# RWKV-6 and a GELU MLP in one kernel: no products of zeros behind the first tile's level bursts, 24 instead of 8 ahead of them, weights loaded later, all loops in another order

## The chip, the core and the metric

The kernel runs on one core of a Trainium2 chip. The metric is the device time of one execution in microseconds. Before the change three executions took 588.85, 590.56 and 590.85 us, a median of 590.56.

Engines are named as the profile names them: PE is the matrix engine (PEld its weight loads), DVE the vector engine, ACT the scalar engine, POOL the general-purpose engine, SP the engine that issues most transfers. Each engine works through its own queue in order. An engine that waits for another one holds up all that is queued behind it.

## The reference

First comes a recurrent attention block (RWKV-6) over 4 batches, 8 heads, 768 steps and 48 columns, then a two-layer MLP with an exact GELU, on 3072 tokens of width 384 with 2048 hidden columns:

```
for t in range(S):
    cur = einsum('bhd,bhe->bhde', u[None] * k_t, v_t)
    y[:, :, t] = einsum('bhd,bhde->bhe', r_t, state + cur)
    state = w_t[:, :, :, None] * state + einsum('bhd,bhe->bhde', k_t, v_t)
x = y.transpose(0, 2, 1, 3).reshape(B * S, H * D)
h = x @ w_in
g = 0.5 * h * (1.0 + erf(h / sqrt(2)))
out = g @ w_out
```

The inputs r, k, v, w and u are float32. The weights w_in and w_out arrive as 64-bit floats, which the kernel reads as 64-bit words and turns into float32 itself.

## The kernel before, in words

The 3072 tokens are worked in eight tiles of 384 tokens, x = 0 to 7. A tile is half the sequence of one batch, all eight heads. Each tile goes through `attention(x, unit)` and then `mlp(x)`.

In the attention, time is cut into chunks of 64 steps. Inside a chunk the sums over earlier steps are made level by level: at level h (1, 2, 4, 8, 16, 32) PE multiplies r of the later half of each block of 2h steps with k of its earlier half. All of a level's products are written by `products` (L445) into one pair of PSUM banks named `d`; such a group is called a burst here. DVE then multiplies r and k by the decays of that level (L494, L505) and copies the burst's block into the matrix `a_sb` through a mask (L516, and L465 for the diagonal), or ACT copies it (L513) where blocks are 16 steps or longer. After the last level k is transposed (`kt_ps`, L685) and copied by ACT (L687), PE makes each chunk's addition to the state (`kv_ps`, L711) and the part inside the chunk (`y_ps`, L752), DVE carries the state from chunk to chunk (`chain_states`, L726 and L731), `fences` (L762, L764) read the finished banks, and PE adds the part from the state (L797). ACT and DVE copy the result into `xT` (L804, L820), a copy `ysb` (L823) and small transfers (L827) fill the rest of `xT`.

Tile 0 is worked as two units, each with half of the heads, so that one unit's DVE work can lie beside the other's PE work. Tile 1 is one unit. Tiles 2 to 7 use another form of the levels, in quarters (L557 to L671).

In the MLP of tile 0, PE makes h one block of 128 hidden columns at a time (L1059, three products a block, in a pool of two banks). ACT's gelu follows in two instructions (L1062, L1064), and PE multiplies by w_out (L1153). From tile 1 on the products are cut in halves in a Strassen-like way (L929, L1073, sums on DVE at L897 and the lines around L1170 to L1196).

The weights come in 16 pieces: eight of w_in and eight of w_out. A piece is loaded by SP into a buffer `raw` (L200, or in three thirds at L205), ACT takes it apart into two halves (`prepare`: L333, L334, L336), and DVE shifts one half (L345) and adds both into the place of the weights (L349). The `gate` form of the loads writes one element of the buffer on DVE first (L204), which delays the issue of the transfer until DVE gets there. The loads of r, k, w of tile 1 have the same gate (L163, L164). The very first transfers (w, k and r of both units at L150, u, v) are issued ahead of all.

PE also runs products of zeros, 128 x 128 by 128 x 512 in bfloat16, whose result nobody reads (`keep_warm`, L225): eight at the start, two behind each burst of tile 0 but the first of each unit (`rest`), and two times three through the stream `warm()`.

The order of work is written out by hand. Every piece of work is a generator that stops at each `yield`. For each tile a string in `PLAN` names which generator goes on next: in tile 0 "." is unit 0, "s" unit 1, "l" the loads with a gate, "c" the weights' conversions, "p" two conversions on their own, "f" the following tile's attention, "w" the load of v, "x" the zeros of `warm()`. In the later tiles "." is the MLP of the tile before, "s" the attention begun in the loop before, "f" the next one, "l" the loads, "c" the weights (tile 1), "x" and "w" sums for the halves. Each engine's queue has its instructions in the order in which the generators wrote them.

## Time and profile before

| | us |
|---|---|
| median of three runs (588.85 to 590.85) | 590.56 |
| the profiled execution | 589.61 |
| its span, first to last instruction | 587.8 |
| PE busy | 571.1 |
| DVE busy | 425.5 |
| ACT busy | 291.2 |
| PE busy in the first 45 us | 33.2 |
| first product of the MLP (h_ps, L1059) | at 44.40 |
| first product with the last piece of w_out (L1153) | at 110.39 |

The profile's times count from the first instruction of the span. The 1.8 us between span and time lie around it. An entry of the timeline gives the start, the length, engine, line, operation, output and inputs with their shape, the number of records, and in brackets how long the engine had been idle and what it had waited for. A float32 product leaves two records, and a few records are missing (of six products of zeros, five may be shown). An entry of the table by stretches gives each engine's busy time in the stretch with the number of instructions, then the granted clock of PE as a share of full speed, the share of the transfer engines and the rate in GB/s.

### The profile page before, as it was taken

How to read it: one execution, taken by the hardware profiler on the slowest of the kernel's cores; microseconds unless marked ns; L12 is line 12 of the kernel's file. 1: busy time of each engine (PE TensorE's matmuls, PEld its weight loads, DVE VectorE, ACT ScalarE, POOL GpSimd, SP SyncE). 2: the span in 40 equal slices, each digit the busy share in tenths (PEclk: the TensorE clock that was granted, in tenths of full speed). 3: DMA queues.
4: the chain of work that ended last, by engine and by line, in shares of the span. 5: the costliest groups of instructions: out<-in, count | busy, mean ns of one | idle time of the engine just before them, and what ended most of it. 6: DMA issues, size and time to landing. Idle time of an engine off the chain costs nothing. (4 is left out here: it accounts for less than half of the span.)

```text
span 587.8 us, 17656 instructions
## 1 busy us (share of the span) xinstructions
PE 571.1 (97%) x7602; PEld 521.4 (89%) x7616; DVE 425.5 (72%) x825; ACT 291.2 (50%) x668; POOL 58.6 (10%) x63
## 2 busy tenths in 40 slices
PE   5789999999999999999999999999999999999997
PEld 3576666799999999999999999999998999999997
DVE  5988968989758975777959986777759987420332
ACT  2368898446362567235462467245561467335400
POOL 3100000013000130012000130002100111003100
PEclk8999999999999999999999999999999999999999
DMA  6749742253032542354122632344224333114201
GB/s 230 221 135 352 265 168 78 79 142 52 5 89 64 157 58 41 90 142 93 26 55 79 151 70 44 86 139 74 27 41 119 86 42 42 29 45 55 28 13 35
DMA packets 62430, 55.09 MB, mean 94 GB/s; under 512 B 32400, under 2 KB 47504, under 8 KB 62352
## 3 DMA queue, kind: packets, MB, share of 16 engines
q1 hardware_dynamic: 50832, 45.62, 25.5%
q0 software_dynamic: 11424, 8.26, 10.8%
q8 instruction: 60, 0.98, 0.7%
q14 instruction: 18, 0.15, 0.1%
q10 hardware_dynamic: 96, 0.07, 0.1%
HBM read 36.24 MB, written 4.72 MB: 70 GB/s over the span
## 5 line engine op out<-in xcount | busy, mean ns | idle before, releaser
L929 PE MATMUL h_ps<-xT,w_in_sb 128*128 128x192 f32 x560 | 111.5, 330 | 0.6 <-DVE o_sb L1196 0.6
L980 POOL DMA_DIRECT2D g<-o_sb x42 | 50.6, 1229 | 478.2 <-ACT o_sb L965 468.9
L929 PEld LDWEIGHTS h_ps<-xT,w_in_sb 128*128 128x128 f32 x560 | 93.0, 190 | 4.7 <-ACT g L961 1.6
L929 PE MATMUL u_ps<-s,w_in_sb 128*128 128x192 f32 x224 | 41.2, 327 | 0.0
L1073 PE MATMUL o_ps<-w_out_sb,g 128*128 128x192 f32 x224 | 39.8, 326 | 0.0
L929 PEld LDWEIGHTS u_ps<-s,w_in_sb 128*128 128x128 f32 x224 | 37.1, 190 | 0.2
L1073 PEld LDWEIGHTS o_ps<-w_out_sb,g 128*128 128x128 f32 x224 | 37.0, 190 | 0.0
L604 ACT COPY a_sb<-d 32x256 f32<-32x256 f32 (+8 forms) x90 | 32.6, 362 | 4.9 <-PE d L588 3.4
L1059 PE MATMUL h_ps<-xT,w_in_sb 128*128 128x384 f32 x96 | 33.2, 494 | 0.0
L452 PEld LDWEIGHTS d<-rkw 64*64 64x64 f32 x1152 | 19.4, 138 | 14.7 <-issue 10.5
L1073 PE MATMUL o_ps<-w_out_sb,f 128*128 128x192 f32 x176 | 32.0, 331 | 0.0
L1073 PE MATMUL o_ps<-t,g 128*128 128x192 f32 x176 | 31.4, 330 | 0.0
L1073 PE MATMUL o_ps<-t,s 128*128 128x192 f32 x176 | 31.2, 328 | 0.0
L1073 PE MATMUL o_ps<-t,e 128*128 128x192 f32 x176 | 30.6, 326 | 0.5 <-issue 0.5
L621 DVE COPY_PREDICATED a_sb<-quarter,d 128x480 f32<-128x480 uint8 (+5 forms) x54 | 23.2, 439 | 10.5 <-PE d L588 9.3
L726 DVE SCALAR_TENSOR_TENSOR st<-st,tot_sb,kv_ps 128x48 f32<-128x48 f32 x160 | 28.9, 258 | 2.6 <-PE kv_ps L711 2.5
L1073 PE MATMUL o_ps<-w_out_sb,e 128*128 128x192 f32 x176 | 30.7, 328 | 0.0
L982 DVE TENSOR_TENSOR g<-g,o_sb 128x384 f32<-128x384 f32 x14 | 7.6, 549 | 31.2 <-ACT o_sb L965 31.1
L1073 PEld LDWEIGHTS o_ps<-t,e 128*128 128x128 f32 x176 | 28.9, 190 | 0.7 <-issue 0.7
L1073 PEld LDWEIGHTS o_ps<-t,g 128*128 128x128 f32 x176 | 28.6, 190 | 0.5
L1073 PEld LDWEIGHTS o_ps<-w_out_sb,f 128*128 128x128 f32 x176 | 28.5, 190 | 0.6
L1073 PEld LDWEIGHTS o_ps<-t,s 128*128 128x128 f32 x176 | 28.8, 190 | 0.2
(163 smaller groups left out, 1171.3 us busy)
## 6 DMA issues: line engine op xcount, KB each, us to landing
rkw<-in_rkw_dram SPq DMA_DIRECT2D x54, 256.0 KB, 3.6
g<-o_sb POOLq DMA_DIRECT2D x42, 192.0 KB, 3.6
raw<-in_w_out_dram SPq DMA_DIRECT2D x8, 768.0 KB, 6.2
v_in<-in_v_dram SPq DMA_DIRECT2D x8, 584.0 KB, 4.6
raw<-in_w_in_dram SPq DMA_DIRECT2D x5, 768.0 KB, 7.5
out_dram<-o_sb SPq DMA_DIRECT2D x20, 192.0 KB, 2.0
rkw<-kx SPq DMA_DIRECT2D x72, 48.0 KB, 2.0
rkw<-in_rkw_dram SPq DMA_DIRECT2D x6, 384.0 KB, 6.2
```

Of the source, the lines that this page charges most:

```text
L452: nc.tensor.matmul(d[half[p], g, n * width:(n + 1) * width], lhsT=kc[half[g], b, i, p], rhs=right(half[g], b, i, p), start=True, stop=True)
L604: nc.scalar.copy(out=at[z, g, first:behind, (a + 1) * h:], in_=d[z, :, :, to] if g == slice(None) else d[z, :, to])
L621: nc.vector.copy_predicated(out=an[:, :, :, :, (a + 1) * h:], mask=mask.to_broadcast(data.shape), data=data)
L726: nc.vector.scalar_tensor_tensor(out=stq[:, q, c], in0=stq[:, q, c - 1] if c else b4[:, q, NC - 1], scalar=totq[:, q, c:c + 1], in1=kvs[q ...
L929: nc.tensor.matmul(o, lhsT=lhsT, rhs=rhs, start=start, stop=True, skip_group_check=True)
L980: nc.gpsimd.dma_start(out=g, in_=z, accum_op=ALU.add)
L982: nc.vector.tensor_add(g, g, z)
L1059: nc.tensor.matmul(h_ps, lhsT=w_in_sb[:, f // FI, j, f % FI * 128:(f % FI + 1) * 128], rhs=xT[:, j, :], start=(j == 0), stop=(j == NJ - 1))
L1073: nc.tensor.matmul(o, lhsT=lhs(j), rhs=rhs(j), start=start and j == 0, stop=(j == HF - 1), skip_group_check=True)
```

## The change

Three things are edited. `keep_warm(8)` at the start becomes `keep_warm(24)`. `products` no longer writes two products of zeros behind a burst of tile 0, so its argument `rest` goes too. And all eight strings of `PLAN` are replaced: the same steps are written in another order.

```
-    0: "l.s....llsl.lssslslss.lc.l.slslls...ssss..lcs.s.s.l.ss..ss..sccs.c.s.llpssslw..cs.ffpcc",
+    0: "..s...lll..sslsslcl.lllcsls.slsp.l.llss.sss..sl.sss..ssc..s.cs..ssc.sl.l.s.sc.cscs.cffwp",
     1: (
-        "..ccswccc.csl.scscs.s.sccwsc.clccs.ccsccc.csc.lscclswwclc.scs.wcssw.ss.cclcsc.ccs.lclccsc."
-        "ccclfccccccfccfcccccfccfccwf.ff......fw.sl.w.x.wx...x..x...xww"
+        "wl.cwcs.c..sslsccc.ccc.sswsccsc.ccl.csccwsl.scscsssccclc.ssscw.sll.cs..l.l.ccsccccffccsccf"
+        "ccccfc.ccccfcccccc.fc..c..cc..lccwwsx.w.w.x..x.x....xww..w"
     ),
     2: (
-        "s.s.....ss....ssw.ws.wl.wsss.wws.s..lsl...lws.w..s.ww....s.s..l..sss.lssss....s..s..s.sls."
-        "llsf.sf.fs..fl.xx.x.fxx"
+        "sss.lsw.w..s....sw..s.w.l..s.sswsss.wl.....sl.w.slw..sswwss....ssss.sssl.s...s....s...s.ls"
+        ".ssllf..sf.fs.ff..xxl..xfxx"
     ),
...
-    keep_warm(8)
+    keep_warm(24)
...
-        def products(bs, right, width, rest=False):
+        def products(bs, right, width):
             d = pair("d")
...
-            if x == 0 and not rest:
-                keep_warm(2)
             return d[:, :, 0:n * width]
...
-                    d = products(range(np_), lambda z, b, i, p: rc[z, b, i, p], C, h == 1)
+                    d = products(range(np_), lambda z, b, i, p: rc[z, b, i, p], C)
```

On the engines' queues this gives, for tile 0: 24 products of zeros ahead of the first burst, and none between the bursts, in sum eight fewer than before. The gate's write for the first third of piece 0 moves on DVE from ahead of the first decay products (L411) to behind the first pair of L494; those of piece 1 move a few instructions ahead. ACT converts piece 1 (L333 to L336) right behind piece 0, ahead of its copies L513, where it stood behind the second L687. DVE's levels of the two units are interleaved otherwise, both chains of states follow each other directly, and the fence of unit 1 stands behind both. On SP the last third of piece 2 is issued ahead of the transfers of `xT`.

For tile 1: on PE the products of level bursts from `kx` stand between h blocks 0 and 1 instead of 1 and 2, and `kt_ps` and `kv_ps` come two h blocks earlier. On ACT the conversion of piece 3 stands ahead of the gelu of block 1, where it stood behind it, and later conversions move against the gelus in the same way; on DVE the pieces 8 and later are added behind the chain of states.

For tiles 2 to 7 single steps move: in tile 2 ACT's L604 copies go ahead of L1115 and L1118, one DVE product L385 goes ahead of L1189, L1192 and L1196, and the first two groups of the level products at L588 are written ahead of a pair of h products.

More of the change, by code (lines that the diff above doesn't have):

```diff
@@ L39 @@
 PLAN = {
-    0: "l.s....llsl.lssslslss.lc.l.slslls...ssss..lcs.s.s.l.ss..ss..sccs.c.s.llpssslw..cs.ffpcc",
+    0: "..s...lll..sslsslcl.lllcsls.slsp.l.llss.sss..sl.sss..ssc..s.cs..ssc.sl.l.s.sc.cscs.cffwp",
     1: (
-        "..ccswccc.csl.scscs.s.sccwsc.clccs.ccsccc.csc.lscclswwclc.scs.wcssw.ss.cclcsc.ccs.lclccsc."
-        "ccclfccccccfccfcccccfccfccwf.ff......fw.sl.w.x.wx...x..x...xww"
-    ),
-    2: (
-        "s.s.....ss....ssw.ws.wl.wsss.wws.s..lsl...lws.w..s.ww....s.s..l..sss.lssss....s..s..s.sls."
-        "llsf.sf.fs..fl.xx.x.fxx"
-    ),
-    3: (
-        "ls.ls....lss..ss.....ss..l.s.lsss.sss.s.s.s.ss..sss..sssssss....s.s..l...s..l.sslslsf.ffs."
-        "..x.lx..xxx"
-    ),
-    4: (
-        "lls.s.sss..s.l.........ssss.....sss.s.ss.s..s.sllss...s.s..l.sss.ss..s.ss...s..sslsll.s..f"
-        ".sf.sf..ff..xx.xflxx"
-    ),
-    5: (
-        "..ss...s..ssl....sls...s.sss..sss..sss.sls...sllss..sssss.s..l..s.s...s.slll..s.ssfsf.fsf."
-        "....xxx.lxx"
-    ),
-    6: (
-        "ss..sss...s.....s.sl..s...l.s.ssls.s.s..s..sssssl......ss.ssss.sl.sl...s.....ss..llsssl.f."
-        "s.fsf.f.f.xx.l.xffxx"
+        "wl.cwcs.c..sslsccc.ccc.sswsccsc.ccl.csccwsl.scscsssccclc.ssscw.sll.cs..l.l.ccsccccffccsccf"
+        "ccccfc.ccccfcccccc.fc..c..cc..lccwwsx.w.w.x..x.x....xww..w"
+    ),
+    2: (
+        "sss.lsw.w..s....sw..s.w.l..s.sswsss.wl.....sl.w.slw..sswwss....ssss.sssl.s...s....s...s.ls"
+        ".ssllf..sf.fs.ff..xxl..xfxx"
+    ),
+    3: (
+        "..s...s...ss...slss...sss.s..ss..s..sss.sl.ssss..ssssss..l..s...s...s.sl.lsl.sllsslf..fs.f"
+        "xxl....xffxffxf"
+    ),
+    4: (
+        "ll....lss.......s....ss....s..sssss.s.sss..lss...l.s.ls.s.s.ssss.s....s....ssls..llsf.sff."
+        "s.ff.xx...xflxx"
+    ),
+    5: (
+        "s......s..s.ls..sss...sss.ssls.lssssl..s....ls.sss..sslss.ss.....s..ss....sssl.s.sllf.sl.f"
+        ".xx...xxfx"
+    ),
+    6: (
+        ".l.s.s.s.s....s...sl.sss....s...s.ssssss.sls.s..lsls....s.s.s.s.sss.ls..s.....ssll..ss.lsf"
+        ".sl.sff.ff...xx.xfxx"
     ),
-    7: "....ss.s...s.s.s....s.sss..ss.ss.sss..s..sss..sssssss......s.s....s..ssss.s...x.x..xxx",
+    7: "sss..ss.......s..s...s.ssss..s.s.sss..ss..sss..sssss..s..s..s...s..s..ssss.s....x.xxx.x",
 }
```

## Prediction

> **What bounds the kernel now.** I read the page's busy shares first, then the busy time by stretches of 15 us, then the timeline of the start, and last the single waits that the trace shows on PE after 45 us.

> ```profile
> span 587.8 us, 17656 instructions
> PE 571.1 (97%) x7602; PEld 521.4 (89%) x7616; DVE 425.5 (72%) x825; ACT 291.2 (50%) x668; POOL 58.6 (10%) x63
> ...
> 15.00:30.00 15.00, 11.48 (x426) 8.06 (x436) 13.92 (x27) 5.03 (x10) 2.88 (x5) 1.00 0.70 214
> 30.00:45.00 15.00, 13.03 (x466) 10.92 (x461) 12.40 (x45) 9.60 (x18) 0.00 (x0) 1.00 0.47 138
> 45.00:60.00 15.00, 15.00 (x255) 9.50 (x255) 13.52 (x17) 11.58 (x22) 0.00 (x0) 1.00 1.02 369
> 180.00:240.00 60.00, 59.27 (x716) 56.51 (x708) 47.62 (x85) 32.14 (x83) 7.23 (x6) 1.00 0.38 80
> ```

> The columns after the stretch's length are busy PE, PEld, DVE, ACT, POOL, then the granted clock. From 45 us PE is busy nearly all the time (59.27 of 60 us is one of the worst later stretches). Before 45 us it is not: in 15 to 30 us it has 11.48 of 15 while DVE has 13.92. So the first tile is set by DVE (and ACT) handing work to PE, and the rest by PE's work. A reorder of loops can win at most the idle time that PE still has there, 0.73 + 0.32 + 0.54 + 0.30 us, about 1.9 us, in the four stretches between 120 and 540 us that have any; it can lose without a bound.

> The start on PE, and the clock in stretches of 2 us:

> ```profile
> 2.29 3.59 PE L225 MATMUL warm<-zeros 128*128 128x512 bf16 x8 [2.29 <-ACT zeros L217]
> 9.43 1.56 PE L452 MATMUL d<-rkw 64*64 64x64 f32 x48 [3.55 <-DMA rkw<-in_rkw_dram]
> 10.74 1.54 PE L452 MATMUL d<-kx,rkw 64*64 64x64 f32 x48
> 13.00 0.93 PE L452 MATMUL d<-rkw 64*64 64x64 f32 x48
> ...
> 21.89 0.93 PE L452 MATMUL d<-rkw 64*64 64x64 f32 x48
> 22.75 0.39 PE L225 MATMUL warm<-zeros 128*128 128x512 bf16 x1
> 23.28 0.93 PE L452 MATMUL d<-rkw 64*64 64x64 f32 x48
> ...
> 10.00:12.00 2.00, 2.00 (x87) 2.00 (x80) 0.56 (x1) 1.12 (x2) 0.00 (x0) 0.50 0.59 233
> 14.00:16.00 2.00, 1.41 (x53) 1.01 (x58) 2.00 (x6) 0.00 (x0) 0.10 (x1) 1.00 0.79 205
> ```

> PE stands 3.55 us until k of the first unit lands; the clock is then at 0.50 for two bursts (1.56 and 1.54 us instead of 0.93). Later bursts follow each other every 1.40 us: DVE's pace, not PE's.

> In the second tile, ACT's order beside PE's:

> ```profile
> 49.25 0.39 ACT L1062 ACTIVATE g<-h_ps 128x256 f32<-128x256 f32 x1
> 49.52 0.30 ACT L1064 ACTIVATE rkw<-h_ps 128x128 f32<-128x128 f32 x1
> 49.67 0.94 ACT L333 ACTIVATE f<-raw 128x768 f32<-128x768 f32 x1
> 50.49 1.06 ACT L334 ACTIVATE e<-raw,two 128x768 f32<-128x768 uint32 x1
> 51.58 1.07 ACT L336 ACTIVATE e<-raw 128x768 f16<-128x768 f32 x1
> ...
> 48.36 1.63 PE L452 MATMUL d<-kx,rkw 64*64 64x64 f32 x96
> 49.92 4.14 PE L1059 MATMUL h_ps<-xT,w_in_sb 128*128 128x384 f32 x12
> ...
> 190.81 2.22 PE L929 MATMUL h_ps<-xT,w_in_sb 128*128 128x192 f32 x12 [0.36 <-DVE o_sb L1196]
> 205.94 1.06 PE L588 MATMUL d<-kx,rkw 64*64 64x96 f32 x40 [0.36 <-DVE kx L563]
> ```

> The gelu of f=1 (49.25 to 49.82) stands ahead of the conversion of weight piece 3 (49.67 to 52.65). The last two lines are waits of PE in the third tile that the new order touches.

> **The change part by part.** Sums are against the profiled execution (589.61 us, 1.8 us of it around the span), which is 0.95 under the median of 590.56; I add differences to the median.

> *24 wide products in front.* The first 8 end at 5.88 at 0.45 us each. The six wide ones from 43.09 to 44.40 cost 0.218 each, so 16 more end at 5.88 + 3.49 = 9.37, just ahead of 9.43, when k is there: they lie in the 3.55 us of idle time and cost nothing. Bounds: nothing, or, if the 16 also took 0.45, an end at 13.1 (3.7 us late). I take nothing, because in the row of before the half clock, begun at 9.43, is over by the burst at 13.00, about 3.5 us of work later, and the first 8 last 3.59. The benefit: two bursts of 0.93 instead of 1.56 and 1.54, 1.2 us earlier for DVE's first L494 pair. If that cover is not there, the same 1.2 us is lost again.

> [...]

> *No wide products behind the bursts.* Twelve pairs, 24 x 0.218 = 5.2 us of PE, go. They stand where PE waits for DVE (11.48 against 13.92 busy of 15), so their time is idle time afterwards: 0 us by itself. What hid them is DVE's pace; what they hid is that the clock might fall (a rival).

> *The start's other order.* DVE's run from the first to the last L494 (11.11 to 34.95) holds about 2.3 us in which it waits for PE (0.47, 0.13, 0.44, 0.43, 0.84). With the early bursts and the new interleaving of the two units, adding up DVE's durations, the last L494 ends at 32.6 to 33.3, 1.7 to 2.3 us earlier. Most of that is given back. The loads of weight pieces 0 and 1 wait for later memsets on DVE (piece 1's last issue at about 20.7; landings took 3.3 to 4.4 us, so about 25). ACT now converts piece 1 (L333, L334, L336, 3.0 us, at 35.40 before) ahead of the L513 copies, so these start at 25.1 + 3.0 = 28.1 (before 27.73) and their first ten end at 31.6 (31.4). Then kt and L687 (second one ends 34.1 to 34.6, before 35.50), kv, both chains of states (2 x 2.0 us) back to back, and unit 1's fence behind both instead of between them, so both L797 groups come one after the other and end at 40.5 to 41.0 (before 41.70). L820's copies stand behind a DVE shift of piece 1 (L345, 0.55) that is hidden while ysb is made (39.57 before). First h product at 43.45 to 44.05, before 44.40: a gain of 0.35 to 0.95. I take 0.35, since PE's gaps "on issue" in this stretch (1.42 at 21 us, 0.96 at 37 us) are in no term of my sum.

> *Second tile, gelu of f=1 behind piece 3.* The plan puts the conversion of piece 3 ahead of this gelu. h of f=3 needs its bank (two banks). ACT: L401 ends 45.6, piece 2 to 48.6, gelu f=0 0.65, piece 3 about 3.05, gelu f=1 0.65: 52.95. PE's side, from first h at 44.05: f=0 2.0, the kx products 1.6, f=1 2.0, f=2 2.05 : 51.65. PE waits 1.3 us. Behind that gelu on ACT stand f=2's gelu and piece 4; behind PE's h all of PE. Bounds: 0.9 (both sides of the start at their early end) to 1.6.

> *Second tile, kt and kv two h blocks earlier.* In before kv waits L687 with 0.30 us to spare, behind kt and one h block. The new place has the same one block between, but gelu, conversion and the L513 pair (0.78 + 0.79) lie closer ahead of L687 on ACT; by adding up, L687 ends at 81.0 where PE is ready at 80.5: 0.5 us (0 to 0.8, one L687). The w_out pieces, each needed 2.6 us after the one before, come later on DVE (5.4 us more DVE work ahead of piece 10, 4.05 us of slack) but stay ahead of PE, which is late itself. Adding all of PE's second tile, the last w_out piece begins at 112.05, before 110.39: +1.65, the start's gain included.

> *Third tile.* L385 (2.19 us) now stands ahead of L1189, L1192 and L1196; L1196 ends at 191.25 rather than 190.76: +0.4 on PE's wait at 190.81 (0 to 0.5). The same move gives DVE 1.3 us of head start at L563, so the 0.36 at 205.94 may go: between -0.36 and +0.8 (PE reaches d 1.3 us earlier in the new order); I take -0.15. ACT's L604 copies ahead of L1115 and L1118 cost 0: ACT stands idle there until PE's product ends. v_in and the loads of the next tile keep their place to within one or two issues on SP, and a tile of time to land in. Tiles 3 to 7: swaps beside slack of 1 us and more, 0 (-1 to +1).

> Sum: +1.65 + 0.4 - 0.15 = +1.9: 590.56 + 1.9 = 592.5.

> **The rivals.** Faster: the 2.3 us that DVE stands in the start come through to ACT's L804 (ends 41.0 instead of 43.3). Then f=3 begins at 41.0 + 9.6 = 50.6, 1.35 us earlier than before, kv's wait goes, and half of the 1.9 us of later idle time with it: 590.56 - 2.35 = 588.2. For it: DVE has the idle time. Against: ACT's DMA issues (2.2 us from 40.08) and L513 stand in between. It decides from an L804 that ends before 41.2.

> The same within 0.3%: the start gains 0.95, PE waits about 1.5 for the gelu (f=3 at 52.6), kv is in time: +0.65, 591.2.

> Much slower, loads: if piece 1 lands late, every us goes through ACT's queue into L513, kt, kv and h. With the 8.9 us that the first raw load took at the start (4.57 to 13.5), it lands 4.6 us later than in my sum: about 597. For it: DMA share 0.91 to 0.93 in 16 to 20 us.

> Much slower, clock: without zeros behind them the bursts fill only 0.93 of each 1.40 us. If the clock falls, they take 1.55; fourteen of them cost 0.15 each (their pace) to 0.62: 2 to 8.7 us, say 596. Against: in before the gaps that were filled are shorter than 1.5 us, and only the 3.55 us one cost the clock.

> [...]

> **How the numbers follow.** Forecast 0.34 (own range 592.3 to 593.5), faster 0.22, same 0.28, late loads 0.11, clock 0.05. 0.3% is 1.77 us, about what a measurement of this kernel can tell from no change. So faster 0.22, same 0.28, slower 0.50. The range reaches from the faster case to between forecast and late loads: 588.2 to 595.5.

> **What would show it.** Right: zeros until about 9.4 without a gap and bursts of 0.93 from the first on; clock 1.00 up to 45 us; last L494 at about 33; first h near 44; one PE wait of 1 us or more on ACT L1064 near 52 us; o's last piece 1 to 2 us later than 110.39. Wrong: clock under 1.00 between 10 and 40 us, first h before 43 or after 45, or a new wait of over 0.5 us behind 120 us.

## The result: 1.7 us slower, as forecast in size, and most of it from a place the forecast had counted as a gain

The changed kernel takes 591.97 us (median of nine executions, 590.61 to 593.42), the kernel before 590.27 us (nine, 588.6 to 590.85). The ratio is 1.0033, with a 95% interval of 1.0019 to 1.0048: 1.1 to 2.8 us slower. The forecast was 592.5 us beside 590.56, +1.9 us. The profiled execution's span went from 587.8 to 590.4 us, +2.6; the rest of this section reads that execution.

The page of the changed kernel, busy shares and the granted clock in 40 slices:

```profile
span 590.4 us, 17655 instructions
PE 572.6 (97%) x7606; PEld 523.3 (89%) x7608; DVE 423.5 (72%) x825; ACT 291.7 (49%) x668; POOL 58.0 (10%) x63
...
PEclk9789999999999999999999999999999999999999
```

PE is busy 1.5 us longer although eight products of zeros are gone, and the clock now sags in the second and third slice (15 to 44 us), where it was full before. By stretches of 15 us and, inside, of 2 us (columns as before: busy PE, PEld, DVE, ACT, POOL, granted clock, transfer share, GB/s):

```profile
15.00:30.00 15.00, 10.46 (x432) 9.53 (x432) 13.72 (x30) 8.44 (x15) 2.26 (x5) 0.77 0.79 259
30.00:45.00 15.00, 11.15 (x390) 10.01 (x385) 10.40 (x38) 3.78 (x8) 0.00 (x0) 0.89 0.26 85
45.00:60.00 15.00, 14.06 (x226) 8.42 (x225) 12.76 (x20) 13.11 (x23) 0.00 (x0) 1.00 0.99 366
...
14.00:16.00 2.00, 0.56 (x34) 0.42 (x26) 1.40 (x6) 0.00 (x0) 0.72 (x2) 1.00 0.83 279
18.00:20.00 2.00, 1.66 (x57) 1.34 (x56) 2.00 (x6) 1.51 (x2) 0.00 (x0) 0.75 0.98 339
20.00:22.00 2.00, 1.41 (x48) 1.22 (x48) 2.00 (x6) 0.00 (x0) 0.00 (x0) 0.50 1.02 372
36.00:38.00 2.00, 0.09 (x8) 0.00 (x1) 1.96 (x13) 0.00 (x0) 0.00 (x0) 1.00 0.00 0
40.00:42.00 2.00, 2.00 (x50) 2.00 (x49) 0.27 (x1) 0.48 (x1) 0.00 (x0) 0.50 0.00 0
```

Twice PE has a poor stretch at full clock (14 to 16 us, 36 to 38 us), and each time the clock is at half some 4 to 6 us later (0.50 in 20 to 22 and in 40 to 42 us). The timeline of PE for the same time (code behind `products` stands two lines higher in the changed kernel, so L797 is L795 here, L752 is L750, L711 is L709, L1059 is L1057):

```profile
2.29 6.84 PE L225 MATMUL warm<-zeros 128*128 128x512 bf16 x24 [2.29 <-ACT zeros L217]
9.06 0.93 PE L452 MATMUL d<-rkw 64*64 64x64 f32 x48
...
17.14 0.93 PE L452 MATMUL d<-rkw 64*64 64x64 f32 x48 [2.58 <-DVE a_sb L514]
22.49 3.86 PE L452 MATMUL d<-rkw 64*64 64x64 f32 x144 [1.08 <-DVE rkw L503]
...
31.80 0.55 PE L709 MATMUL kv_ps<-v_in,kx 64*64 64x48 f32 x21
33.99 0.61 PE L709 MATMUL kv_ps<-v_in,kx 64*64 64x48 f32 x26 [1.64 <-issue]
38.00 0.91 PE L750 MATMUL y_ps<-a_sb,v_in 64*64 64x64 f32 x43 [1.91 <-issue]
39.06 3.77 PE L795 MATMUL y_ps<-rkw,st 64*64 64x64 f32 x78 [0.15 <-DVE fence L762]
45.92 1.53 PE L1057 MATMUL h_ps<-xT,w_in_sb 128*128 128x384 f32 x4 [0.18 <-PE warm L225]
48.21 0.91 PE L1057 MATMUL h_ps<-xT,w_in_sb 128*128 128x384 f32 x2 [0.76 <-DMA xT<-ysb]
50.61 6.19 PE L1057 MATMUL h_ps<-xT,w_in_sb 128*128 128x384 f32 x18
...
115.83 2.38 PE L1071 MATMUL o_ps<-w_out_sb,rkw 128*128 128x192 f32 x13
```

The reader can follow the loss. The first burst is early and at full clock, as meant. Then kv is interrupted for 1.64 us, y for 1.91 us ("issue": PE waits for nothing that the profile shows), L795 takes 3.77 us for 78 of its 80 records at half clock, where its two groups took 1.33 and 1.66 us before, and the first h product begins at 45.92, 1.52 later than before (44.40). Another 0.76 goes to a late transfer of `xT`, and 0.5 to PE itself, which is busy 69.14 us from there to the first product of L1071, where it was busy 68.65 before; the last was not followed up. Behind that, blocks 1, 2 and 3 of h follow each other without a gap (50.61 to 56.73): the wait for the gelu that the forecast had put there does not occur. At the first product of L1071 the kernel is 2.78 us late (115.83 against 113.05, L1073 before), and at the end 2.6. Tiles 2 to 7 give back about 0.2. The rows of the kernel before for these comparisons:

```profile
38.19 1.33 PE L797 MATMUL y_ps<-rkw,st 64*64 64x64 f32 x40
40.04 1.66 PE L797 MATMUL y_ps<-rkw,st 64*64 64x64 f32 x40 [0.52 <-DVE fence L762]
44.40 4.03 PE L1059 MATMUL h_ps<-xT,w_in_sb 128*128 128x384 f32 x12
...
113.05 5.14 PE L1073 MATMUL o_ps<-w_out_sb,rkw 128*128 128x192 f32 x30
```

The two waits on PE in tile 2 that the forecast named:

```profile
193.48 2.22 PE L927 MATMUL h_ps<-xT,w_in_sb 128*128 128x192 f32 x12 [0.23 <-DVE o_sb L1194]
...
206.88 1.88 PE L586 MATMUL d<-kx,rkw 64*64 64x96 f32 x80
```

The first went from 0.36 to 0.23 instead of growing by 0.4, the second is gone.

### The profile page after: what moved, and what is told of

The parts are those of the page before. It is cut to its first block, busy times and chain, and to the rows that moved or that the text cites. A ratio compares the mean times of both kernels' runs of the same rounds, so it can differ in the third digit from the quotient of the medians.

```text
span 590.4 us, 17655 instructions
## 1 busy us (share of the span) xinstructions
PE 572.6 (97%) x7606; PEld 523.3 (89%) x7608; DVE 423.5 (72%) x825; ACT 291.7 (49%) x668; POOL 58.0 (10%) x63
## 3 DMA queue, kind: packets, MB, share of 16 engines
q1 hardware_dynamic: 50832, 45.62, 25.1%
## 5 line engine op out<-in xcount | busy, mean ns | idle before, releaser
L1071 PE MATMUL o_ps<-w_out_sb,g 128*128 128x192 f32 x224 | 39.8, 326 | 0.0
L1071 PEld LDWEIGHTS o_ps<-w_out_sb,g 128*128 128x128 f32 x224 | 37.0, 190 | 0.0
L1057 PE MATMUL h_ps<-xT,w_in_sb 128*128 128x384 f32 x96 | 33.6, 497 | 0.9 <-DMA xT<-ysb 0.8
L1071 PE MATMUL o_ps<-w_out_sb,f 128*128 128x192 f32 x176 | 32.0, 331 | 0.0
L1071 PE MATMUL o_ps<-t,g 128*128 128x192 f32 x176 | 31.2, 330 | 0.0
L1071 PE MATMUL o_ps<-w_out_sb,e 128*128 128x192 f32 x176 | 31.1, 328 | 0.0
L1071 PE MATMUL o_ps<-t,s 128*128 128x192 f32 x176 | 31.0, 328 | 0.0
L1071 PE MATMUL o_ps<-t,e 128*128 128x192 f32 x176 | 30.4, 326 | 0.0
L452 PEld LDWEIGHTS d<-rkw 64*64 64x64 f32 x1152 | 21.1, 148 | 10.2 <-issue 4.2
L1071 PEld LDWEIGHTS o_ps<-t,g 128*128 128x128 f32 x176 | 28.6, 190 | 0.5
L1071 PEld LDWEIGHTS o_ps<-w_out_sb,f 128*128 128x128 f32 x176 | 28.6, 190 | 0.5
L1071 PEld LDWEIGHTS o_ps<-w_out_sb,e 128*128 128x128 f32 x176 | 28.7, 190 | 0.3
L1071 PEld LDWEIGHTS o_ps<-t,s 128*128 128x128 f32 x176 | 28.8, 190 | 0.2
L1071 PEld LDWEIGHTS o_ps<-t,e 128*128 128x128 f32 x176 | 28.9, 190 | 0.0
```

Source lines behind the costliest of these rows:

```text
L452: nc.tensor.matmul(d[half[p], g, n * width:(n + 1) * width], lhsT=kc[half[g], b, i, p], rhs=right(half[g], b, i, p), start=True, stop=True)
L1057: nc.tensor.matmul(h_ps, lhsT=w_in_sb[:, f // FI, j, f % FI * 128:(f % FI + 1) * 128], rhs=xT[:, j, :], start=(j == 0), stop=(j == NJ - 1))
L1071: nc.tensor.matmul(o, lhsT=lhs(j), rhs=rhs(j), start=start and j == 0, stop=(j == HF - 1), skip_group_check=True)
```

## The experiments

Two theories stood against each other. S, the forecast's: the loss is made in the second tile, by the gelu and kv. T, read from the profile above: it is made in tile 0, by the order there, by PE's waits on issue and by the fallen clock. Twelve kernels were run. Differences are those of the ratio to runs of the kernel before on the same chip. In kernels whose strings were rewritten the lines stand 18 or so lower (L1039 there is L1057 in the changed kernel).

### Which part of the change costs: tile 0's string, the other strings, the zeros

Tile 0's string from before in the changed kernel (`PLAN[0]` old, one "c" put ahead of `PLAN[1]` so that the weights' steps stay equal in number):

```
-    0: "..s...lll..sslsslcl.lllcsls.slsp.l.llss...
+    0: "l.s....llsl.lssslslss.lc.l.slslls...ssss...
```

> The changed kernel with the string of tile 0 from before (one step of the weights, which that string has fewer, put at the start of tile 1's); zeros as in the changed kernel. Theory S (the forecast's: the loss is made in the second tile, where gelu f=1 stands behind piece 3 and kv comes early, 1.3 + 0.5 us): still 1.3 to 2 us slower than before. Theory T (the loss is made in tile 0: PE waits for instructions inside kv and y, 1.64 and 1.91 us, and its clock falls to half in two stretches): within 0.7 us of before or faster, first h product before 44.8.

Measured: ratio 1.0013 (0.9989 to 1.0036), +0.8 us with an interval from -0.6 to +2.1, which holds the numbers of both theories: the time does not decide here. First h is at 42.01, as T has it, and PE waits 0.48 us for the gelu:

```profile
42.01 2.10 PE L1039 MATMUL h_ps<-xT,w_in_sb 128*128 128x384 f32 x6
...
50.21 2.20 PE L1039 MATMUL h_ps<-xT,w_in_sb 128*128 128x384 f32 x6 [0.48 <-ACT rkw L1044]
```

So the wait that S names exists in this execution, where h is early, but it is 0.48 and not 1.3. From the first h to the first product of the halves (L1053 there) this execution takes 69.4 us, the kernel before 68.65: +0.8 for the whole of tile 1's new order.

The reverse, tile 0's new string and the new zeros alone (`PLAN[1]` to `PLAN[7]` as before):

```
+    0: "..s...lll..sslsslcl.lllcsls.slsp.l.llss...
     1: as before, without its first "c"; 2 to 7 as before
```

> Only tile 0's string and the zeros from the changed kernel; tiles 1 to 7 in the order of before. Theory S: 0.3 to 1 us faster than before. Theory T: 1.2 to 2.5 us slower than before, with first h near 45.9 and PE idle on issue inside kv and y.

Measured: 1.0026 (1.001 to 1.0043), +1.5 us (0.6 to 2.5), where S had a gain of 0.3 to 1: S fails, and tile 0 with its zeros is enough for a loss of about the size of the whole change. T is right on the time and on the gaps, but not on the place. In the profile first h is at 44.35 (T said 45.9), no later than in the kernel before:

```profile
33.55 0.61 PE L691 MATMUL kv_ps<-v_in,kx 64*64 64x48 f32 x26 [0.78 <-issue]
...
37.83 0.91 PE L732 MATMUL y_ps<-a_sb,v_in 64*64 64x64 f32 x43 [2.19 <-issue]
38.62 2.32 PE L777 MATMUL y_ps<-rkw,st 64*64 64x64 f32 x78
...
44.35 0.81 PE L1039 MATMUL h_ps<-xT,w_in_sb 128*128 128x384 f32 x2
```

The clock is full here when PE adds the part from the state (L777), which takes 2.32 us and not 3.77. So the 1.52 us at first h in the changed kernel's profile belong to that drop of the clock in the main; where this execution loses its time was not found.

The new zeros with the old order:

```
-    keep_warm(8)
+    keep_warm(24)
-            if x == 0 and not rest:
-                keep_warm(2)
```

> The order of before in all tiles; 24 zeros in front and none behind the bursts. Theory S: 0.3 to 1.2 us faster than before (the two bursts at half clock are gone). Theory T: the clock falls to half where a window of 3.4 us is no more than half busy, and the points where PE waits for instructions move, so between 0.5 us faster and 1 us slower; the granted clock shows a stretch at 0.50 between 13 and 40 us.

Measured: 1.0016 (0.9991 to 1.0042). The median hides two kinds of execution. Time and mean granted clock of its twelve:

```
587.06 (0.997)  587.81 (0.997)  587.81 (1.000)  588.13 (0.997)  588.60 (0.997)
589.44 (0.994)  591.00 (0.994)  591.83 (0.988)  592.55 (0.991)  593.06 (0.988)  593.11 (0.986)  593.93 (0.991)
```

One window of 3.41 us at half clock lowers the mean over 588 us by 0.003: the profile of the kernel before has one (9.36 to 12.77 us) and a mean of 0.997, that of the changed kernel three and 0.991. With at most one such window the mean is 587.88, 1.5 us under the kernel before at the same clock (589.36, 27 of 29 executions in that job); with two or more it is 592.13, 2.8 over. The kernel before falls under 0.996 in 2 executions of 29 (in 6 of 29 and in 1 of 27 in the other two jobs), this one in 7 of 12. Here dropping the zeros behind the bursts is a gain of 1.5 us when the clock holds and a loss of 2.8 when it doesn't. The kernel `new_but_plan0` has the same zeros and tile 0 and differs in tiles 1 to 7 alone: its median in the same job is 589.85 against 590.22, and with at most one half window 588.69 (6 of 12) against 587.88. So the strings of tiles 1 to 7 cost about 0.8 us where the clock holds, and nothing that shows in the medians.

This grouping also bounds what the clock explains in the new order, and there it is little. In the changed kernel the four executions with at most one half window average 591.62, the five others 592.12; with tile 0's new string alone it is 590.68 (4) and 590.98 (8). At a clock that holds, tile 0's new string costs about 590.68 - 587.88 = 2.8 us beside the old one with the same zeros. No profile of such an execution was taken, so what makes up these 2.8 us is not shown.

In the profiled execution of the old order with the new zeros:

```profile
34.29 0.30 PE L732 MATMUL y_ps<-a_sb,v_in 64*64 64x64 f32 x6
36.99 0.85 PE L732 MATMUL y_ps<-a_sb,v_in 64*64 64x64 f32 x42 [2.40 <-issue]
37.64 3.79 PE L777 MATMUL y_ps<-rkw,st 64*64 64x64 f32 x78
```

The new order with the old zeros (8 in front, two behind):

> The order of the changed kernel in all tiles; 8 zeros in front and two behind the bursts, as before. Theory S: 1.9 us slower than before or more (the early clock is lost too). Theory T: if the half clock after 15 us is the larger part, the clock stays at 1.00 after 13 us and the time is within 0.7 us of before; if the waits for instructions are, it stays 1 to 2 us slower.

Measured: 595.98 us, 1.0108 (1.0085 to 1.013), +6.4. That is far outside T's numbers. S had 1.9 us or more, but the loss is not where S puts it: first h is already 5.8 us late, at 50.16. The profile has one gap of 2.74 us on issue inside the second kv (37.74 to 40.48), the fence after it, a window 20% busy, and L779 at half clock (4.07 us):

```profile
40.48 0.20 PE L693 MATMUL kv_ps<-v_in,kx 64*64 64x48 f32 x1 [2.74 <-issue]
...
43.04 4.07 PE L779 MATMUL y_ps<-rkw,st 64*64 64x64 f32 x78 [1.31 <-DVE fence L744]
...
50.16 2.10 PE L1041 MATMUL h_ps<-xT,w_in_sb 128*128 128x384 f32 x6
```

The four medians of this job (before 589.28, new zeros 590.22, tile 0's new string with the new zeros 590.8, all new strings with the old zeros 595.98) show that the two edits hang together: the edit of the zeros costs little in the old order and saves about 5 us in the new one (+6.4 with the old zeros, +1.7 in the changed kernel).

### What the zeros do, in front and behind

The kernel before with 24 in front, the rest untouched:

```
-    keep_warm(8)
+    keep_warm(24)
```

> The kernel before with 24 instead of 8 zeros in front, two behind the bursts as before, old order. Theory C (the clock is granted by how busy a window of 3.4 us was, and zeros behind the bursts hold it up): the first bursts take 0.93 us, the clock stays at 1.00 to the end of tile 0 in the profile, and the time is 0 to 1.2 us under before with a spread as small as before's. [...]

Measured: 589.97 us, 1.0005 (0.9986 to 1.0025), no difference. The clock is 1.00 in nine executions of eleven and never under 0.997; the first bursts take 0.93 and 0.88. That is theory C on the clock: this kernel differs from the old order with the new zeros by the pairs behind the bursts alone, and there 7 of 12 executions are under 0.996. But the 1.3 us gained at the first bursts shrink to 0.5 at the first h (43.88) and to nothing that can be told in the time.

The changed kernel with the pairs behind the bursts put back:

> The changed kernel with the two zeros behind each burst put back (24 in front stay). Theory C: no stretch at half clock between 15 and 26 us; since the zeros also stand in the queue ahead of the next burst (0.39 us each time), the time is between 1 us faster than the changed kernel and the same. Rival (new order with 8 in front and zeros behind was 6.4 us slower than before because of the zeros behind, not because of the front): 4 us or more slower than before.

Measured: 594.74 us, 1.0085 (1.0058 to 1.0112), +5.0. Here the rival was right and I was wrong: in the new order the zeros stand in PE's queue ahead of bursts that would be ready. With them the last burst begins at 31.39, without them at about 29 (the first one at 10.07 and 9.06). The gap on issue then falls into the second kv, and the clock still drops later, after that gap (a window 35% busy):

```profile
10.07 0.93 PE L452 MATMUL d<-rkw 64*64 64x64 f32 x48
...
31.39 0.93 PE L452 MATMUL d<-rkw 64*64 64x64 f32 x48
...
39.40 0.49 PE L711 MATMUL kv_ps<-v_in,kx 64*64 64x48 f32 x18 [2.59 <-issue]
```

So zeros behind the bursts are no cure for the new order, and the new order is no gain with them.

Old string of tile 0, new strings for the rest, 24 in front and two behind:

> Old string of tile 0, new order of tiles 1 to 7, 24 zeros in front and two behind the bursts. Theory C: the clock stays at 1.00, the spread is as small as before's. With the gelu of block 1 waiting behind piece 3 as the only loss (0.5 to 1.1 us) and the early bursts as the gain (0.5): 0 to 0.8 us slower than before. If the new order of tiles 2 to 7 is worth anything by itself, it shows here as 0.5 us faster or more.

Measured: 590.35 us, 1.0024 (0.9999 to 1.0049), +1.4 us (-0.1 to +2.9), where theory C had 0 to 0.8. The clock stayed (0.999 or more in nine of twelve), yet two executions took 593.5 and 595.0, so the spread was not small. The new order of tiles 1 to 7 shows no gain by itself.

The changed kernel with 16 in front:

```
-    keep_warm(24)
+    keep_warm(16)
```

> The changed kernel with 16 instead of 24 zeros in front. The forecast's step (24 cost nothing since k lands at 9.43): first burst no earlier than 9.0. Rival (with the weights loaded later k lands at 8.5, as the new order with 8 zeros showed, and 24 zeros stand in its way): the first burst begins at 8.3 to 8.7, 0.4 to 1.5 us earlier than with 24, at full clock; the time falls by at most that, 0 to 1 us under the changed kernel's.

Measured: 591.3 us, 1.0028 (1.0003 to 1.0052). PE's first burst:

```profile
9.12 0.93 PE L452 MATMUL d<-rkw 64*64 64x64 f32 x48 [0.35 <-DMA rkw<-in_rkw_dram]
```

k lands at 9.12 here (at 8.49 in the new order with 8 in front), and PE stands only 0.35 us before. The forecast's "cost nothing" holds in the profile of the changed kernel (24 zeros in 6.84 us, first burst at 9.06). In `new_with_zeros_behind` and `new_half_the_instructions` the 24 zeros take 7.85 and 7.90 us and the first burst begins at 10.07 and 10.12; if k landed near 9.12 there too, they cost about 1 us (an estimate).

### The gelu behind piece 3, by itself

The kernel before, with one move in tile 1's string:

```
-        "..ccswccc.csl.scscs.s...
+        ".ccs.wccc.csl.scscs.s...
```

> The kernel before with one move in tile 1's string: h block 1 and its gelu go behind the first weight conversion and the kx products, as in the changed kernel, so ACT does piece 3 ahead of gelu f=1. Forecast's price: PE waits 1.3 us for the gelu near 52 us, 1.0 to 1.6 us slower than before. Rival (a wait that PE has room for): PE waits under 0.6 us there, within 0.6 us of before.

Measured: 590.9 us, 1.0024 (1.0005 to 1.0043), +1.4 us (0.3 to 2.5), as the forecast priced it. But the profiled execution does not show it as a wait of 1.3 us: PE waits 0.27 on that gelu, behind a tile 0 that was itself disturbed (a window 48% busy, then half clock, first h at 46.82). With a mean clock of 0.996 or more its eight executions average 590.82 against 589.69 for the kernel before, so +1.1 is left. The time agrees with the forecast's price, the wait with its rival (under 0.6); that the 1.1 us are this wait in executions with an early h is not shown.

### What the gaps on issue are, and whether they set the time

Kv and y of tile 0 from half the instructions (upper halves of the words as bfloat16, so the output of tile 0 is coarse); y is changed in the same way as kv:

```
+        def short(z):
+            if x:
+                return z
+            return z.bitcast(BF16).rearrange("p (a two) -> p a two", two=2)[:, :, 1]
...
-                        nc.tensor.matmul(kv_ps[half[g], p, i * D:(i + 1) * D], lhsT=k_t(b, i, p, g),
-                                         rhs=vs(b, i, g)[half[p], 0:D], start=True, stop=True)
+                        nc.tensor.matmul(kv_ps[half[g], p, i * D:(i + 1) * D], lhsT=short(k_t(b, i, p, g)),
+                                         rhs=short(vs(b, i, g)[half[p], 0:D]), start=True, stop=True)
```

> The changed kernel; in tile 0 alone kv and y are made from the upper halves of the float32 words read as bfloat16 (a product is then one pass instead of two, half the PE instructions; the values are cut to 8 bits of mantissa, so the output is coarse). Theory I (PE's idle time on issue inside kv and y is the fetch of instructions, 256 at a time): the gaps of 1.64 and 1.91 us go or shrink to under 0.8 us together, and first h is 1.5 to 3 us earlier than in the changed kernel (45.92). Rival (the gaps are something else, contention of transfers or ACT's and DVE's copies): gaps of the same size at the same place, first h within 0.8 us of 45.92.

Measured: 591.81 us, 1.0036 (1.0012 to 1.006).

```profile
34.64 0.21 PE L714 MATMUL kv_ps<-v_in,kx 64*64 64x48 bf16 x3 [0.70 <-issue]
...
35.44 0.37 PE L755 MATMUL y_ps<-a_sb,v_in 64*64 64x64 bf16 x24
39.26 4.07 PE L800 MATMUL y_ps<-rkw,st 64*64 64x64 f32 x78 [3.45 <-DVE fence L767]
```

The gaps shrink from 3.55 to 0.70 us, as theory I had it. The size alone is weak evidence: in the next kernel, with the same halves, the gap in kv is 1.67 us, as long as in the changed kernel. What ties the gaps to PE's instructions is their place, 256 of them apart (after 1473 and 1729 in the changed kernel, last section); with half of them the count at which the gap in y would come is no longer reached inside y. But first h, 36.7 us behind the first burst, is no earlier than in the changed kernel (36.9). PE now waits 3.45 us for the fence instead, its window is 25% busy, and L800 runs at half clock. So the gap in y of the changed kernel covers a wait for DVE's two chains of states and costs nothing by itself; the one in kv delays those chains, for which DVE waits 2.22 us there.

I tried to hold the clock up in that wait with 20 products of zeros:

```
                 ys.append((y, None if split else y_ps))
+            if x == 0 and not split:
+                for _ in range(20):
+                    nc.tensor.matmul(kv_ps[:, 0, 384:512], lhsT=zeros[:, 0:128], rhs=zeros[:, 0:128], ...)
```

> The changed kernel with kv and y of tile 0 in bfloat16 halves (coarse output, half the PE instructions), and 20 products of zeros (128 columns) behind the second unit's y, where PE stood 3.45 us for the fence. Theory C (L797 ran at half clock, 4.07 us instead of 2.7, because the window before it was 25% busy): the zeros keep the window busy, L797 takes under 3.2 us, first h comes 0.8 to 2 us earlier relative to the first burst than without them (36.7 us behind it). Rival (L797 and h are late for another reason, the fence or the transfers of xT): the same 36.5 to 37 us.

Measured: 593.17 us, 1.0055 (1.0033 to 1.0078). The zeros stood in the wrong place: the second unit's y is written first, so they ran at 34.80, ahead of the first unit's kv, and PE still stood 3.90 us for the fence (one whole window without work, then half clock, L803 3.81 us). The rows:

```profile
34.46 0.21 PE L714 MATMUL kv_ps<-v_in,kx 64*64 64x48 bf16 x3 [1.67 <-issue]
...
34.80 1.29 PE L760 MATMUL kv_ps<-zeros 128*128 128x128 bf16 x20
...
40.50 3.81 PE L803 MATMUL y_ps<-rkw,st 64*64 64x64 f32 x78 [3.90 <-DVE fence L768]
```

The run doesn't decide between C and its rival for that place; that test was not made.

The kernel before with 24 in front and tile 1's first products behind the first h block (`PLAN[0]` with one "f" fewer, `PLAN[1]` with an "s" after its first step):

> The kernel before with 24 zeros in front, zeros behind the bursts kept, and tile 1's first group of level products moved from ahead of the first h block to behind it: 96 records, 192 PE instructions fewer ahead of h. If PE sets the start of h there (instructions at their own pace, 1.5 us of d): h 0.5 to 1.2 us earlier and 0.3 to 1 us faster than before. If ACT's copy L804 sets it: h at most 0.2 us earlier, the same time.

Measured: 595.21 us, 1.0087 (1.0055 to 1.0119), +5.1: slower, where both theories had it equal or faster. First h came at 45.07 after 1.43 us of waiting for ACT's copy, and block 1 waited 2.25 us on issue ahead of its first product, from 48.80 on, a place where PE had no wait before; the clock fell there too. The place fits the count of the last section. The last packet of instructions ahead of the end of this wait (51.05) begins at 48.73, 9.8 us after the one before it; why it comes so late is open.

## Why the forecast was right, and where its steps were wrong

The number and the sign hold: +1.9 forecast, +1.7 (1.1 to 2.8) measured. That is luck, since errors in both directions cancel. In the profiles, up to the first h the forecast had -0.35 and +1.52 was measured; from there to the first product of L1071 it had +2.0 and got +1.26, of which 0.76 is a wait that it did not name; behind that it had +0.25 and got -0.2. (The terms that it names for the second tile, -0.35 + 1.3 + 0.5, add up to 1.45; 0.2 of its 1.65 has no term.)

- The start's order, taken as a gain of 0.35: the step that failed. It was +1.52 in the profile. Up to the last L492 (L494 before; it ends at 32.55, forecast 32.6 to 33.3) and the second L685 (ends at 33.41, forecast 34.1 to 34.6) the addition held, even with some room. It failed behind: kv was torn by 1.64 us of waiting on issue; DVE's chain began at 34.77, hardly earlier than before (34.94); and L795 ran at half clock. The forecast had taken the low end because such gaps were "in no term of my sum"; it should have given them a term. By the executions with a clock that holds, tile 0's new string costs 2.8 us.
- "No wide products behind the bursts", "0 us by itself": wrong too, and in both directions. Their time was not idle time: without them (and with 24 in front) the old order is 1.5 us faster where the clock holds, and in the new order leaving them out saves about 3 us (+5.0 with them, +1.7 without). But the clock held with them: without them 7 of 12 executions of the old order have two half windows or more, and these are 4.2 us longer than the others; with them and the same 24 in front it is none of 11. The rival with this mechanism had a chance of 0.05. In the changed kernel's profile the clock fell in two stretches, not for the whole of tile 0, and over its executions the fall explains little of the +1.7.
- 24 zeros in front: right in the profile. No gap, first burst at 9.06 and 0.93 us long, no half clock at 9.4.
- The gelu behind piece 3, 1.3 us: 0 in the changed kernel's profile, 0.48 with an early h, 0.27 by itself (with +1.4 in time). The wait exists, but in the changed kernel PE was late itself: the gelu of block 1 ended at 54.55, and PE was at the end of block 2 only at about 54.7.
- Kv early in tile 1, 0.5 us: nothing; kv follows h at 82.20 without a gap. Instead `xT` came 0.76 late, which no term held: its transfers were issued behind a ysb that was 1.65 late, and ACT needed 2.94 us for its three issues (2.18 before).
- Tile 2, +0.25: about -0.5 there, the waits 0.23 and none.

The rival of late loads fell: piece 1 was there at 24.29, before the 25 of the sum. Two of the three things that the forecast would take as showing it wrong happened: a clock under 1.00 between 10 and 40 us and a first h after 45. The total alone would have hidden that.

That the clock falls, and after which windows, is shown by the table in the last section. Open are what the fall costs in the changed kernel, what else makes its tile 0 slow when the clock holds, and the exact length of each gap on issue, since the same place shows gaps of different length.

## What to carry to other kernels

Products that seem only to fill idle time may be worth more than their time: here the clock was under 0.996 in 7 of 12 executions without the pairs behind the bursts and in none of 11 with them. Before such products are dropped, add up how busy PE is without them in each stretch of the length at which the traces show the clock change (3.41 us here), and count those at half or less: here the next window was at half after all 13 windows of 42% or less, and after 6 of 10 of 45 to 54%. The old order with the new zeros has two kinds of executions (587.88 and 592.13 us), so compare executions grouped by their granted clock beside the median. The same grouping also tells when the clock is not the cause. And when a run agrees with a forecast, still read the steps: here 1.9 us too little in tile 0 met 1.2 us too much behind it.

## What the runs showed of the hardware

All figures here are counted from the fourteen profiles of this case (its two kernels and the twelve experiments): the granted clock, the matrix records and the packets are their entries.

```
at full clock   busy 0 to 42%    13 windows: the next at half in all 13
                busy 45 to 54%   10 windows: the next at half in 6, full in 4
                busy 56% or more  the next full in all
at half clock   busy 62 to 69%    4 windows: the next still half in all 4
                busy 80 to 84%    4 windows: the next full in 3
                busy 87% or more  the next full in all
```

The window ahead of the drop at 9.36 in the kernel before had no product at all, but a drop did not need that: in the changed kernel the two windows ahead of a drop were 50% and 40% busy. Single gaps of 1.9 to 2.7 us were enough there and in the experiments (1.91 in the changed kernel, 2.74 in `new_plan_old_zeros`), and in one window two of 0.91 and 1.06 us (`new_but_plan0`, 42% busy).

**The waits on issue lie 256 PE instructions apart, or a multiple of that.** The page of the changed kernel's profile has 60 packets and 0.98 MB of instructions, 16 384 bytes each in the trace. PE has 15 214 of the 17 655 instructions in the trace, 254 for each packet if all packets were PE's, which no view shows. In the changed kernel the gaps on issue come after 1473 and after 1729 of PE's instructions. The same holds everywhere: the 40 waits of PE on issue of 0.3 us or more between 13 and 60 us, in all fourteen profiles, come after 705, 961, 1217, 1473, 1729, 1985 or 2241 PE instructions, to within one (PE's semaphore instructions are counted with them, products missing from a trace by their weight loads). With eight zeros fewer in front, 16 PE instructions, the gap in kv comes 16 instructions later in kv: behind 29 records of products instead of 21. So in these profiles a gap belongs to a place in PE's program, not to a time or an operand. Those of 0.7 us or more end 2.2 to 2.8 us after a packet begins (in the changed kernel at 33.99 and 38.00, with packets at 31.73 and 35.48). In the answer on transfers between 33 and 39 us of the changed kernel, the gap in y (36.1 to 38.0) has no other traffic beside it:

```profile
GB/s 96 96 41 123 300 423 300 382 342 328 369 314 205 137 41 0 109 0 0 0 0 0 0 0 0 0 0 0 0 0 0 0 0 0 0 0 0 0 0 0
...
q8 instruction: 1, 0.02, 1.2%
```

A burst of 24 float32 products of 64 by 64 is 96 PE instructions in 0.93 us, so 256 would take about 2.5 us at that pace (an estimate), while packets in these profiles begin 3.3 us apart or more (3.75 and 3.67 us around these gaps). That PE waits for these packets is a reading of the places and times above; no view names it as the cause. What decides when the next packet is asked for was not found: for the gaps of 0.7 us or more it began between 1.9 us before PE ran dry and 0.4 us after.
